# Four small loads on 32 partitions each become two on 64, and SyncE waits for the last eight loads in a no-operation

## The chip, the cores and the metric

The kernel runs on one core of one Trainium2 chip. The metric is the device time of one execution in microseconds (us); lower is better. A profile of one execution gives the span from its first to its last recorded instruction, which is a little shorter than the device time.

## The reference

The kernel computes one decoding step of a layer with two branches. Branch A is attention over a sliding window of the last 4096 cached positions, with 32 query heads on 8 key and value heads of size 128. Branch B is a gated linear unit with 1792 hidden values. A scalar gate mixes the two. Everything is bf16, and there is one token with 512 values.

```python
x = A_x                                              # 1 x 1 x 512
g = sigmoid((x * gate_w).sum(-1))
q = (x @ wq).reshape(1, 1, 32, 128)                  # wq 512 x 4096
k, v = last W = 4096 positions of the caches         # each 8 x 4096 x 128
p = softmax(q . k * 128 ** -0.5)
a = (p . v).reshape(1, 1, 4096) @ wo                 # wo 4096 x 512
h = sigmoid(x @ w_gate) * (x @ w_up)                 # both 512 x 1792
b = h @ w_down                                       # 1792 x 512
out = g * a + (1 - g) * b
```

With one token there is no reuse of weights or caches. All 30.67 MB of weights, keys and values are read once from HBM.

## The kernel before

SyncE issues all the large loads, in the order in which they are used: wq, four loads of keys, w_gate, w_up, four loads of values, two loads of wo, and four pieces of w_down whose sizes fall to the end. The row p of w_up in SBUF holds the four rows 4p to 4p+3 of the matrix. Its main load takes all of each partition but the last three quarters of the fourth row. Those 128 remainders of 1344 values (2688 B) go into a tile of their own, `wx_sb`, of 64 partitions and two halves h, through four small loads.

```python
P = 128; DC = 4; F = 1792; FQ = 448; NP = 64; NJ = 14
WD_SPLIT = (0, 8, 11, 13, 14)
dq = nc.sync
wq_sb = big.tile([P, DC, HQ * DH], BF16, name="wq_sb", tag="big")
dq.dma_start(wq_sb[:], wq_v)

def load_pair(t, cache, a, n0=0, n1=NP):
    dq.dma_start(t[:, n0:n1, :]..., cache[0, 2 * a:2 * a + 2, SBASE:SBASE + W, :]...)

kn = []
for a in range(HP):                                  # 4 loads of keys, 2 MB each
    kn.append(blk.tile([P, NP, P], BF16, name="kn", tag="blk"))
    load_pair(kn[a], A_k_cache, a)
# ... wg_sb
FX = 3 * FQ
LM = DC * F - FX
dq.dma_start(wu_sb[:].rearrange("p c f -> p (c f)")[:, 0:LM],
             B_w_up.rearrange("(p c) f -> p (c f)", c=DC)[:, 0:LM])
wx_sb = const.tile([64, 2, FX], BF16, name="wx_sb")
wx_v = B_w_up.rearrange("(h b j i c) f -> h b i j c f", h=2, b=2, j=4, i=8)[:, :, :, :, DC - 1, F - FX:F]
for h in range(2):
    for b in range(2):
        dq.dma_start(wx_sb[32 * b:32 * b + 32, h, :], wx_v[h, b])

vv = []                                              # 4 loads of values, in the buffers of the keys
for a in range(HP):
    vv.append(blk.tile([P, NP, P], BF16, name="vv", tag="blk"))
    load_pair(vv[a], A_v_cache, a)
# ... wo_sb in two loads
for j0, j1 in zip(WD_SPLIT[:-1], WD_SPLIT[1:]):
    dq.dma_start(wd_sb[:, j0:j1, :], wd_v[:, j0:j1, :])
```

The order of the small rows on the partitions has to agree with the order of the values of x that multiply them. These are picked from x with the same pattern, put on the partitions by two tiny matmuls, and used as stationary operand where the product with w_up comes to the last row:

```python
for h in range(2):
    nc.vector.tensor_copy(xp[:, h, :].rearrange("o (b i j) -> o b i j", b=2, j=4),
                          xr[:, 0, :].rearrange("o (h b j i c) -> o h b i j c", h=2, b=2, j=4, i=8)[:, h, :, :, :, DC - 1])
    nc.tensor.matmul(xx_ps[:, h:h + 1], lhsT=xp[:, h, :], rhs=ident[0:1, 0:1], ...)
# ...
if w == 1 and c == DC - 1 and j >= 1:
    for h in range(2):
        nc.tensor.matmul(g_out, lhsT=xx[:, h:h + 1].to_broadcast([64, 32]),
                         rhs=wx_sb[:, h, (j - 1) * FQ:j * FQ], start=False, stop=(h == 1))
```

After the loads come the scores (DVE transposes the keys, PE multiplies them with the queries), the softmax, the product with the values (`pv_ps`), the product with w_up, and at the end the two output products, which add to one tile `a_ps`: 64 matmuls with wo and 28 with w_down. DVE and ScalarE copy half of `a_ps` each into `res`, and ScalarE issues the output transfer.

Completion of the loads is counted on eight semaphores in turn. A load that takes a semaphore first waits for the load that had it before, eight loads earlier.

Of the kernel before, what the change touches and what calls it, by code (L numbers as in the profile page):

```python
# [17 lines left out]
def kernel(  # L18
# [14 lines left out]
    nc = tc.nc  # L33
# [3 lines left out]
    DC = D // P  # L37
# [5 lines left out]
    W = min(4096, max(256, Sk // 4))  # L43
    KB = W // P
    SBASE = Sk - W
    F = B_w_gate.shape[1]
    NJ = F // P
    N_OUT = A_wo.shape[1]
    NC_O = HQ * DH // P
# [7 lines left out]
    NP = 2 * KB  # L57
# [15 lines left out]
    xr = const.tile([1, 2, D], BF16, name="xr")  # L73
    nc.scalar.dma_start(xr[:, 0, :], A_x[0, :, :])
    nc.scalar.dma_start(xr[:, 1, :], gate_w.rearrange("(o n) -> o n", o=1))

    dq = nc.sync
    wq_sb = big.tile([P, DC, HQ * DH], BF16, name="wq_sb", tag="big")
    wq_v = A_wq.rearrange("(p c) n -> p c n", c=DC)
    dq.dma_start(wq_sb[:], wq_v)  # L80


    def load_pair(t, cache, a, n0=0, n1=NP):
        dq.dma_start(t[:, n0:n1, :].rearrange("p n d -> p (n d)"),  # L84
                     cache[0, 2 * a:2 * a + 2, SBASE:SBASE + W, :]
                     .rearrange("y (x n) d -> x y n d", n=NP)[:, :, n0:n1, :].rearrange("x y n d -> x y (n d)"))

    kn = []
    for a in range(HP):
        kn.append(blk.tile([P, NP, P], BF16, name="kn", tag="blk"))  # L90
        load_pair(kn[a], A_k_cache, a)
# [5 lines left out]
    FX = 3 * FQ  # L97
# [1 line left out]
    dq.dma_start(wu_sb[:].rearrange("p c f -> p (c f)")[:, 0:LM],  # L99
                 B_w_up.rearrange("(p c) f -> p (c f)", c=DC)[:, 0:LM])  # L100
    wx_sb = const.tile([64, 2, FX], BF16, name="wx_sb")
    wx_v = B_w_up.rearrange("(h b j i c) f -> h b i j c f", h=2, b=2, j=4, i=8)[:, :, :, :, DC - 1, F - FX:F]
    for h in range(2):
        for b in range(2):
            dq.dma_start(wx_sb[32 * b:32 * b + 32, h, :], wx_v[h, b])

    vv = []
    for a in range(HP):
        vv.append(blk.tile([P, NP, P], BF16, name="vv", tag="blk"))
        load_pair(vv[a], A_v_cache, a)  # L110

    wo_sb = big.tile([P, NC_O, N_OUT], BF16, name="wo_sb", tag="big")
    wo_v = A_wo.rearrange("(p c) n -> p c n", c=NC_O)
    for c0 in (0, NC_O // 2):
        dq.dma_start(wo_sb[:, c0:c0 + NC_O // 2, :], wo_v[:, c0:c0 + NC_O // 2, :])

    wd_sb = w14.tile([P, NJ, N_OUT], BF16, name="wd_sb", tag="w14")
    wd_v = B_w_down.rearrange("(p j) n -> p j n", j=NJ)
    for j0, j1 in zip(WD_SPLIT[:-1], WD_SPLIT[1:]):
        dq.dma_start(wd_sb[:, j0:j1, :], wd_v[:, j0:j1, :])  # L120


    identf = const.tile([P, P], F32, name="identf")
# [26 lines left out]
    xx_ps = ps_m.tile([64, 2], F32, name="xx_ps", tag="m")  # L150
    xp = const.tile([1, 2, 64], BF16, name="xp")
    for h in range(2):
        nc.vector.tensor_copy(xp[:, h, :].rearrange("o (b i j) -> o b i j", b=2, j=4),
                              xr[:, 0, :].rearrange("o (h b j i c) -> o h b i j c", h=2, b=2, j=4, i=8)[:, h, :, :, :, DC - 1])
        nc.tensor.matmul(xx_ps[:, h:h + 1], lhsT=xp[:, h, :], rhs=ident[0:1, 0:1],
                         start=True, stop=True, skip_group_check=True)
    xT = const.tile([P, DC], BF16, name="xT")
# [216 lines left out]
```

## Time and profile before

| | |
|---|---|
| device time | 80.44 us, median of 3 runs (80.42 to 80.53) |
| span of the profiled execution | 78.7 us, run of 80.39 us |
| granted TensorE clock, mean | 0.973 |
| PE, DVE, ACT busy | 52.5, 38.8, 10.9 us |
| read from HBM | 30.67 MB, 390 GB/s over the span |

The page names PE (TensorE matmul), PEld (its weight load), DVE (VectorE), ACT (ScalarE), POOL (GpSimd), and SPq (SyncE's sequencer, which issues the loads). L105 is line 105 of the kernel, the four small loads. L369 is the end of the program. A DMA's line is named by its destination and source. The page's DMA issues say what each load carries, in the order in which they were costliest:

```profile
## 6 DMA issues: line engine op xcount, KB each, us to landing
kn<-in_A_k_cache_dram SPq DMA_DIRECT2D x4, 2048.0 KB, 27.2
vv<-in_A_v_cache_dram SPq DMA_DIRECT2D x4, 2048.0 KB, 19.1
wq_sb<-in_A_wq_dram SPq DMA_DIRECT2D x1, 4096.0 KB
wo_sb<-in_A_wo_dram SPq DMA_DIRECT2D x2, 2048.0 KB
wg_sb<-in_B_w_gate_dram SPq DMA_DIRECT2D x1, 1792.0 KB
wu_sb<-in_B_w_up_dram SPq DMA_DIRECT2D x1, 1456.0 KB
```

The four small loads have 84.0 KB each. A chip core has 16 DMA engines; a large load is spread over all of them, and the DMA share in the views is the mean busy share of the 16.

### The profile page before, as it was taken

The numbers are of one execution on the slowest core, as the hardware profiler recorded it, in microseconds if no ns is written. First come the engines' busy times: TensorE is split into PE (matmuls) and PEld (weight loads), VectorE is DVE, ScalarE is ACT, GpSimd is POOL, SyncE is SP. The second block draws the span as 40 slices with busy tenths as digits, with TensorE's granted clock in tenths as the row PEclk, the third lists the DMA queues.
The fourth block names the chain that finished last, engine by engine and source line by source line (L and its number), as shares of the span: only waits on it lengthen the run. The fifth ranks groups of instructions, "written<-read, shape, count | busy, mean of one in ns | idle before, by whom it ended". The sixth has DMA issues, their size and how long they took to land.

```text
span 78.7 us, 798 instructions
## 1 busy us (share of the span) xinstructions
PE 52.5 (67%) x314; PEld 23.6 (30%) x314; DVE 38.8 (49%) x52; ACT 10.9 (14%) x20; POOL 3.3 (4%) x10
## 2 busy tenths in 40 slices
PE   0200094999905788898887307999996799567650
PEld 0200041344302333333332202344341345345420
DVE  1600920029869999999986349962000000690020
ACT  2400000247651000000002191000000002000010
POOL 7900000000000000000000000000000000000000
PEclk9999999999999999999999995699999999999997
DMA  7779799999999999999999999999999999999710
GB/s 184 300 316 533 316 483 391 408 425 458 441 408 416 425 474 416 386 437 417 438 410 426 441 416 441 408 433 441 416 433 433 424 425 433 416 391 409 290 42 1
DMA packets 2616, 30.71 MB, mean 390 GB/s; under 512 B 307, under 2 KB 438, under 8 KB 822
## 3 DMA queue, kind: packets, MB, share of 16 engines
q1 hardware_dynamic: 2608, 30.67, 92.9%
q8 instruction: 2, 0.03, 0.2%
q10 hardware_dynamic: 6, 0.00, 0.0%
HBM read 30.67 MB, written 0.00 MB: 390 GB/s over the span
## 4 chain that ended last, share of the span: by engine, by line
DMA 93%; SPq 2%; PE 1%; DVE 1%; issue 0%
DMA wd_sb<-in_B_w_down_dram 36%; DMA kn<-in_A_k_cache_dram 32%; DMA vv<-in_A_v_cache_dram 24%; SPq L84 2%; PE a_ps L290 1%; DVE res L341 1%; SPq L80 0%
## 5 line engine op out<-in xcount | busy, mean ns | idle before, releaser
L299 PE MATMUL pv_ps<-vv,eT 128*32 128x512 bf16 x64 | 15.9, 405 | 4.1 <-DVE eT L271 2.8
L227 PE MATMUL S_ps<-kT,qbig 128*128 128x512 bf16 x64 | 15.2, 378 | 5.0 <-DVE qbig L216 2.8
L188 DVE STREAM_TRANSPOSE kT<-kn 128x2048 f32<-128x2048 f32 x8 | 17.8, 2282 | 0.0
L227 PEld LDWEIGHTS <-qbig 128*128 128x128 bf16 x64 | 6.1, 97 | 14.1 <-issue 4.2
L299 PEld LDWEIGHTS <-eT 128*32 128x32 bf16 x64 | 6.2, 102 | 12.9 <-issue 4.2
L200 PE MATMUL q_ps<-wq_sb,xT 128*128 128x512 bf16 x32 | 8.8, 442 | 1.2 <-DMA wq_sb<-in_A_wq_dram 1.2
L318 DVE TENSOR_TENSOR oT<-o_ps,rb 128x32 bf16<-128x32 f32 x1 | 0.2, 191 | 13.5 <-PE o_ps L316 13.5
L205 DVE STREAM_TRANSPOSE qtT<-q_sb 128x512 f32<-128x512 f32 x4 | 2.7, 700 | 6.9 <-ACT q_sb L202 6.9
L182 PE MATMUL S_ps<-ident,other 2*128 2x512 bf16 x4 | 2.0, 611 | 5.8 <-DVE other L140 5.8
L202 ACT CAST q_sb<-q_ps 128x512 bf16<-128x512 f32 x8 | 4.7, 585 | 7.0 <-PE q_ps L200 7.0
L200 PEld LDWEIGHTS <-xT 128*128 128x128 bf16 x32 | 3.5, 111 | 6.8 <-issue 4.2
L290 PE MATMUL a_ps<-wo_sb,oY 128*1 128x256 bf16 x64 | 3.8, 272 | 1.5 <-DMA wo_sb<-in_A_wo_dram 1.2
L290 PEld LDWEIGHTS <-oY 128*1 128x1 bf16 x64 | 2.7, 83 | 3.1 <-issue 1.4
L271 DVE STREAM_TRANSPOSE eT<-e_sb 128x1024 bf16<-128x1024 bf16 x2 | 2.4, 1224 | 1.9 <-ACT e_sb L269 1.9
L254 ACT ACTIVATE sge<-gu_ps 128x448 f32<-128x448 f32 x1 | 0.5, 543 | 18.9 <-PE gu_ps L243 18.9
L309 ACT COPY pv_sb<-pv_ps 128x512 f32<-128x512 f32 x1 | 0.6, 585 | 17.7 <-PE pv_ps L299 17.7
L341 DVE CAST res<-a_ps 1x256 bf16<-1x256 f32 x1 | 0.4, 412 | 5.2 <-PE a_ps L290 5.2
L281 DVE RECIPROCAL sg<-sge 128x448 f32<-128x448 f32 x1 | 3.0, 2952 | 0.0
L165 DVE TENSOR_TENSOR gpr<-xr 1x512 f32<-1x512 bf16 x1 | 0.7, 679 | 4.6 <-DMA xr<-in_gate_w_dram 4.6
L249 DVE TENSOR_REDUCE pm<-S_ps 128x1 f32<-128x1024 f32 x2 | 2.4, 1208 | 0.9 <-PE S_ps L227 0.9
L290 PE MATMUL a_ps<-wd_sb,hT 128*1 128x256 bf16 x28 | 2.1, 271 | 0.8 <-DMA wd_sb<-in_B_w_down_dram 0.8
L148 PE MATMUL xt_ps<-ident,xr 1*128 1x1 bf16 x4 | 0.3, 165 | 3.5 <-POOL ident L126 3.5
(62 smaller groups left out, 31.0 us busy)
## 6 DMA issues: line engine op xcount, KB each, us to landing
kn<-in_A_k_cache_dram SPq DMA_DIRECT2D x4, 2048.0 KB, 27.2
vv<-in_A_v_cache_dram SPq DMA_DIRECT2D x4, 2048.0 KB, 19.1
wq_sb<-in_A_wq_dram SPq DMA_DIRECT2D x1, 4096.0 KB
wo_sb<-in_A_wo_dram SPq DMA_DIRECT2D x2, 2048.0 KB
wg_sb<-in_B_w_gate_dram SPq DMA_DIRECT2D x1, 1792.0 KB
wu_sb<-in_B_w_up_dram SPq DMA_DIRECT2D x1, 1456.0 KB
wd_sb<-in_B_w_down_dram SPq DMA_DIRECT2D x1, 1024.0 KB
wd_sb<-in_B_w_down_dram SPq DMA_DIRECT2D x1, 384.0 KB
```

The lines of the kernel that those rows point to most:

```text
L84: dq.dma_start(t[:, n0:n1, :].rearrange("p n d -> p (n d)"), cache[0, 2 * a:2 * a + 2, SBASE:SBASE + W, :] .rearrange("y (x n) d -> x y n ...
L182: nc.tensor.matmul(S_ps[u // 2][:, u % 2, :], lhsT=other[:].rearrange("p o y u -> p (o y u)"), rhs=ident[0:2, 0:2].rearrange("p (o y) -> p ...
L188: nc.vector.transpose(t[:].bitcast(F32), kn[a][:, v * KB:(v + 1) * KB, :] .rearrange("p n d -> p (n d)").bitcast(F32))
L200: nc.tensor.matmul(q_ps[:], lhsT=xT[:, c:c + 1].to_broadcast([P, P]), rhs=wq_sb[:, c, ks], start=(c == 0), stop=(c == DC - 1))
L202: nc.scalar.copy(q_sb[:, ks], q_ps[:])
L205: nc.vector.transpose(qtT[:].bitcast(F32)[:, kq], q_sb[:].bitcast(F32)[:, kq])
L227: nc.tensor.matmul(S_ps[v][:, hb, :], lhsT=q_st[:, a, dhi, :, t], rhs=k_v[:, hb * 16:(hb + 1) * 16, dhi, :, t], start=False, stop=(a == HP ...
L249: nc.vector.tensor_reduce(pm2[:, v:v + 1], S_ps[v][:].rearrange("p a b -> p (a b)"), axis=AX.X, op=ALU.max)
L271: nc.vector.transpose(eT[:, :, v * KB:(v + 1) * KB, :].rearrange("p a n r -> p n a r"), e_sb[:, v, :].rearrange("p (n a r) -> p n a r", a= ...
L281: nc.vector.reciprocal(sg[:], sge[:])
L290: nc.tensor.matmul(a_ps[32 * i:32 * i + 1, i, 0:HN], lhsT=lhsT, rhs=rhs[:, i * HN:(i + 1) * HN], start=start, stop=stop)
L299: nc.tensor.matmul(pv_ps[32 * a:32 * a + 32, :, :], lhsT=eT[:, a, 4 * m:4 * m + 4, :].rearrange("p n r -> p (n r)"), rhs=vv[a][:, 4 * m:4 ...
```

## The change

The four small loads of 32 partitions become two of 64, one for each half h. The eight values of i remain the slowest dimension of the source, so that the rows stay on eight DMA engines, now with eight rows for each engine and load. The order of the values of x follows. The second part collects the load instructions in a list and puts a no-operation into SyncE's stream, after the last issue, that depends on the last eight of them (two of vv, two of wo, four of w_down); the closing waits of the program then need not name these loads again. The purpose is fewer loads and fewer waits at the end. What is computed stays the same.

```diff
+    loads = []
...
     def load_pair(t, cache, a, n0=0, n1=NP):
-        dq.dma_start(t[:, n0:n1, :].rearrange("p n d -> p (n d)"),
...
+        loads.append(dq.dma_start(t[:, n0:n1, :].rearrange("p n d -> p (n d)"),
...
     wx_sb = const.tile([64, 2, FX], BF16, name="wx_sb")
-    wx_v = B_w_up.rearrange("(h b j i c) f -> h b i j c f", h=2, b=2, j=4, i=8)[:, :, :, :, DC - 1, F - FX:F]
+    wx_v = B_w_up.rearrange("(h j i c) f -> h i j c f", h=2, j=8, i=8)[:, :, :, DC - 1, F - FX:F]
     for h in range(2):
-        for b in range(2):
-            dq.dma_start(wx_sb[32 * b:32 * b + 32, h, :], wx_v[h, b])
+        dq.dma_start(wx_sb[:, h, :], wx_v[h])
...
-        dq.dma_start(wd_sb[:, j0:j1, :], wd_v[:, j0:j1, :])
+        loads.append(dq.dma_start(wd_sb[:, j0:j1, :], wd_v[:, j0:j1, :]))
+
+
+    seen = dq.nop()
+    for load in loads[-8:]:
+        tc.add_manual_dep(seen.ins, load.ins.name,
+                          mybir.DependencyInfo(mybir.DependencyClass.Sync, mybir.DependencyReason.DATA), reason="loads ended")
...
     for h in range(2):
-        nc.vector.tensor_copy(xp[:, h, :].rearrange("o (b i j) -> o b i j", b=2, j=4),
-                              xr[:, 0, :].rearrange("o (h b j i c) -> o h b i j c", h=2, b=2, j=4, i=8)[:, h, :, :, :, DC - 1])
+        nc.vector.tensor_copy(xp[:, h, :].rearrange("o (i j) -> o i j", i=8),
+                              xr[:, 0, :].rearrange("o (h j i c) -> o h i j c", h=2, j=8, i=8)[:, h, :, :, DC - 1])
```

More of the change, by code (lines that the diff above doesn't have):

```diff
@@ L83, in load_pair @@
     def load_pair(t, cache, a, n0=0, n1=NP):
-        dq.dma_start(t[:, n0:n1, :].rearrange("p n d -> p (n d)"),
-                     cache[0, 2 * a:2 * a + 2, SBASE:SBASE + W, :]
-                     .rearrange("y (x n) d -> x y n d", n=NP)[:, :, n0:n1, :].rearrange("x y n d -> x y (n d)"))
+        loads.append(dq.dma_start(t[:, n0:n1, :].rearrange("p n d -> p (n d)"),
+                                  cache[0, 2 * a:2 * a + 2, SBASE:SBASE + W, :]
+                                  .rearrange("y (x n) d -> x y n d", n=NP)[:, :, n0:n1, :].rearrange("x y n d -> x y (n d)")))
     kn = []
@@ L114 @@
     for c0 in (0, NC_O // 2):
-        dq.dma_start(wo_sb[:, c0:c0 + NC_O // 2, :], wo_v[:, c0:c0 + NC_O // 2, :])
+        loads.append(dq.dma_start(wo_sb[:, c0:c0 + NC_O // 2, :], wo_v[:, c0:c0 + NC_O // 2, :]))
     wd_sb = w14.tile([P, NJ, N_OUT], BF16, name="wd_sb", tag="w14")
```

## The prediction

> **What bounds the kernel now.** I read the shares of the chain that ended last, then the DMA lines, then that chain in order of time, and last the same span in half-microsecond windows. From the page, the shares by engine and by line, and the DMA totals:
>
> ```profile
> DMA packets 2616, 30.71 MB, mean 390 GB/s; under 512 B 307, under 2 KB 438, under 8 KB 822
> q1 hardware_dynamic: 2608, 30.67, 92.9%
> DMA 93%; SPq 2%; PE 1%; DVE 1%; issue 0%
> DMA wd_sb<-in_B_w_down_dram 36%; DMA kn<-in_A_k_cache_dram 32%; DMA vv<-in_A_v_cache_dram 24%; SPq L84 2%; PE a_ps L290 1%; DVE res L341 1%; SPq L80 0%
> ```
>
> 93% of the chain is transfer, nearly all on the queue of SyncE; PE is busy 67% of the span and DVE 49%, neither is the limit. The end of the chain in order of time (start, length, what):
>
> ```profile
> 46.84 28.67 DMA wd_sb<-in_B_w_down_dram
> 75.51 0.04 issue
> 75.55 0.66 PE a_ps L290 x6
> 76.20 0.40 DVE res L341
> ```
>
> The last piece of w_down lands at 75.51 us of a span of 78.7 us. Six matmuls, the copy of the result and the output transfer follow, 3.2 us that this change does not touch. So the time moves with the landing of the last load and with little else. The windows (length, busy PE, PEld, DVE, ACT, POOL, PE clock, DMA share, GB/s) show how the stream runs in its middle and how it ends:
>
> ```profile
> 56.00:58.00 2.00, 1.96 (x10) 0.69 (x8) 0.00 (x0) 0.00 (x0) 0.00 (x0) 1.00 1.00 426
> 72.50:73.00 0.50, 0.50 (x14) 0.41 (x10) 0.00 (x0) 0.00 (x0) 0.00 (x0) 1.00 1.07 428
> 73.50:74.00 0.50, 0.10 (x2) 0.09 (x3) 0.00 (x0) 0.00 (x0) 0.00 (x0) 1.00 0.77 295
> 74.00:74.50 0.50, 0.50 (x12) 0.40 (x10) 0.00 (x0) 0.00 (x0) 0.00 (x0) 1.00 0.64 242
> 74.50:75.00 0.50, 0.50 (x13) 0.31 (x10) 0.00 (x0) 0.00 (x0) 0.00 (x0) 1.00 0.63 229
> 75.00:75.50 0.50, 0.36 (x6) 0.15 (x3) 0.00 (x0) 0.00 (x0) 0.00 (x0) 1.00 0.24 82
> ```
>
> The DMA engines are full (share 1.00, 426 GB/s, that is 26.6 GB/s for each of 16) until about 73.2 us, and then only some of them work for two more microseconds. Which ones? The 307 packets under 512 B are completion marks: 17 loads from SyncE on 16 engines give 272, the four small loads of w_up on 8 engines give 32, the three transfers on the other queue give 3, together 307. On 16 engines the small loads would have given 64, together 339. So wx_sb moves on 8 engines alone: 128 rows of 2688 B are 344 KB, 43 KB for each of the eight, 43 KB / 26.6 GB/s = 1.6 us of work that the other eight do not have. The engines with the small rows are those that end last, at 75.2 to 75.5 us; the packet records of the trace put six of the others at 73.7 to 74.0. The remaining two end with the late ones: two packets of instructions of 16 KB (q8 on the page) hold up one engine each. **Anything that lengthens the small rows therefore lengthens the kernel almost one for one; shortening them helps only until those two engines are left.**
>
> The waits of SyncE's own queue, at the end of the program and at the v loads (total, times, longest), and its issues (start, time):
>
> ```profile
> SPq L369 <- DMA wd_sb<-in_B_w_down_dram: 23.3, 3, 21.8
> SPq L84 <- DMA kn<-in_A_k_cache_dram: 8.4, 2, 4.2
> SPq L369 <- DMA out_dram<-res: 1.1, 1, 1.1
> SPq L369 <- DVE res L341: 1.1, 1, 1.1
> ```
>
> ```profile
> 12.95 10.46 SPq L105 DMA_DIRECT2D wx_sb<-in_B_w_up_dram  x4
> 27.70 14.67 SPq L84 DMA_DIRECT2D vv<-in_A_v_cache_dram  x4
> ```
>
> SyncE is through with its last issue at 51.7 us and has nothing to do but wait. At the end it is held by the w_down pieces, then by DVE's copy, then by the output, in that order.
>
> [...]
>
> **The change part by part.** *Rows and engines.* The bytes are the same, 344 KB on 8 engines, 16 rows each. Before, load b of half h puts rows 4i to 4i+3 of a block of 32 partitions on engine i[...]. After, 64 partitions are cut in 8 for the 8 values of i. [...] I take it that engine i gets partitions 8i to 8i+7. [...] No run here shows this split of 64; it is my inference.
>
> *Its cost.* A 2688 B row takes 0.103 to 0.107 us in the packet records, so 16 rows take 1.67 us. [...] They are not in step: the eight engines reach the small rows between 39.59 and 39.94 us, neighbours in time some 0.1 us apart. In a set of four rows (0.42 us alone) the one that is ahead by d has d to itself and shares the rest, so a set takes 0.84 - d. With d = 0.05 to 0.15 four sets cost 4 x (0.27 to 0.37) = 1.1 to 1.5 us. About 1.3 us[...].
>
> *Two loads fewer.* Each of the eight engines writes two marks less: the packet records show about 0.01 us each, so -0.02 us. SyncE saves two issues of 0.7 us (10.46 us for four include the waits between), not on the path. The slots of eight semaphores shift by two: the first v load waited for the third k load until 27.6 us, now for the first one and for DVE's second transposition, which ends about 26.8; so it is issued about 0.9 us earlier. The later v loads also wait for DVE or an earlier k load. All this is hidden: vv lands 19 us after its issue because some 14 us of queue are ahead of it (its landing at 46.8 less 5 us for its own 128 KB per engine).
>
> *The no-operation.* Its eight waits come after the last issue, on SyncE alone, and are over with the last w_down piece at 75.5. Until 76.6 DVE's copy holds SyncE anyway, and until about 77.6 the output. Before, the same waits stood in the closing block, also ahead of those two. One wait instruction and a branch of perhaps 0.1 us (my guess) then have 1.1 us to hide in: 0.
>
> *Sum.* 80.44 - 0.02 + 0 + (0, or about 1.3) = 80.4 or 81.7.
>
> **The rivals.** *No sharing, nothing moves:* 80.4. For it: all rows still go to the same 8 engines with the same bytes, and the diff intends own partitions. [...] *Sharing in step:* 82.0 to 82.1, 2% slower; against it the 0.1 us offsets. *The closing waits come out:* if SyncE's last waits cost time after the output, taking six of the eight away would give some tenths, 80.1; but the waits view shows the output as the last to release it. *The earlier v loads fill gaps:* only if the stream starved, and from 38 to 72 us the share stays at 0.93 or more: 0 to -0.1. PE taking over as the bound: it would need to lose its slack before w_down; it follows the v loads, and these shift by no more than w_down does.
>
> **Range and chances.** [...] Between 80.4 and 81.7 I put 81.2 us; 80.2 to 82.1 should hold it 8 times in 10. Slower by over 2% (above 82.05) needs sharing in step: 0.13. Faster by over 2% (below 78.8) has no source, since two engines end at 75.4 without the small rows: 0.02. Within 2%: 0.85.
>
> **What would show it.** 2600 packets with 291 under 512 B confirm eight engines and two loads. Sharing shows in the window 39.5 to 43.5 us: DMA bytes fall well under 426 GB/s, the first v load's landing goes from 46.8 to about 48, and the last w_down landing to about 76.8 with a longer stretch at half share ahead of it. Without sharing the last landing stays at 75.5 and the half-share stretch at 2 us. If the stretch from the last landing to the end differs from 3.2 us, I was wrong on the no-operation. If the landing moves earlier than 75.2, I was wrong on what ends last.

## The result, and the profile after

| | before | after |
|---|---|---|
| device time, median | 80.51 us (80.42 to 81.83, 6 runs) | 81.46 us (81.25 to 81.87, 6 runs) |
| span of the profiled execution | 78.7 us | 79.6 us |
| first load (wq) landed | 12.95 us | 13.21 us |
| last piece of w_down landed | 75.51 us | 76.38 us |
| from there to the end of the span | 3.2 us | 3.2 us |

The ratio of after to before is 1.0125, with an interval of 1.0098 to 1.0152. Some executions of most of these kernels take 1.5 to 2.2% longer than the others of the same kernel (81.83 us here, of the kernel before); medians and ranges have them in, ratios do not. The change costs 1.0 us of device time, and what was meant to save loads and waits saves nothing. The DMA totals and the shares of the chain that ended last, from the page of the changed kernel:

```profile
DMA packets 2600, 30.71 MB, mean 386 GB/s; under 512 B 291, under 2 KB 422, under 8 KB 806
...
DMA 77%; PE 13%; DVE 6%; ACT 1%; issue 0%
DMA wd_sb<-in_B_w_down_dram 36%; DMA vv<-in_A_v_cache_dram 25%; DMA wq_sb<-in_A_wq_dram 16%; PE q_ps L206 12%; DVE kT L194 3%; DVE qbig L222 2%; DVE qtT L211 1%; PE a_ps L296 1%; ACT q_sb L208 1%; DVE res L347 1%
```

There are 16 packets less, all of them completion marks: two loads fewer on eight engines each. The bytes are the same. The chain now passes through PE and DVE for 19%, where before it was 93% transfer. That is no new bound. It is another route back through the same early stretch, as the chain in order of time shows (start, length, what):

```profile
25.49 2.32 DVE kT L194
...
27.83 19.87 DMA vv<-in_A_v_cache_dram
...
47.72 28.66 DMA wd_sb<-in_B_w_down_dram
76.38 0.04 issue
76.43 0.64 PE a_ps L296 x6
77.07 0.40 DVE res L347
```

The first v load is now released by DVE's transposition of the keys (L194) instead of by the landing of a k load, and so the walk back goes through DVE and PE. The load itself still waits in a full queue for most of its 19.87 us. From the v landing on, both chains are alike: 28.66 us here and 28.67 us before to the last landing, then the same tail. So the loss is already there at 47.70 us, where before the landing was at 46.84. The windows of the changed kernel over the small rows and over the end (length, busy PE, PEld, DVE, ACT, POOL, PE clock, DMA share, GB/s):

```profile
39.50:41.50 2.00, 1.71 (x9) 0.70 (x8) 2.00 (x2) 0.00 (x0) 0.00 (x0) 1.00 1.06 348
41.50:43.50 2.00, 2.00 (x23) 0.78 (x21) 1.11 (x2) 0.00 (x0) 0.00 (x0) 1.00 1.04 360
...
75.50:76.00 0.50, 0.50 (x12) 0.31 (x9) 0.00 (x0) 0.00 (x0) 0.00 (x0) 1.00 0.51 180
```

And the same four microseconds of the kernel before:

```profile
39.50:41.50 2.00, 1.71 (x9) 0.68 (x7) 1.60 (x2) 0.00 (x0) 0.00 (x0) 1.00 1.06 425
41.50:43.50 2.00, 1.32 (x19) 0.33 (x16) 1.38 (x2) 0.54 (x1) 0.00 (x0) 1.00 1.02 434
```

The DMA share is over 1.00 in all four lines: on average no engine is idle, before or after. Yet the changed kernel moves 348 and 360 GB/s where before it was 425 and 434. Engines that are busy and move less are being held in their packets, whose times follow below. The loss is (77 + 74) GB/s x 2 us = 302 KB, which at the stream's 426 GB/s is 0.7 us. Outside this stretch the streams run alike: in the packet records of the trace the changed kernel is 28 KB behind the kernel before at 39.4 us, 331 KB at 43.5 us and 339 KB at 60 us. At the end, half of the engines are still busy at 75.5 to 76.0 us (share 0.51), when the kernel before is through.

In the packet records, the small rows of 2688 B take 107 ns each before, and 134 ns on average after; along one engine they swing between 107 and about 200 ns. The first 16 KB packets of v that follow take up to 948 ns, against 614 ns undisturbed. These records are what the experiments below are read by, together with the windows. They do not name the engine, but one small row follows another closely (in both kernels the next starts, in the median, 3 ns ahead of the recorded end of the one before), and so an engine can mostly be followed.

### The profile page after: what moved, and what is told of

It is laid out like the page before. It is cut to its first block, busy times and chain, and to the rows that moved or that the text cites. A ratio compares the mean times of both kernels' runs of the same rounds, so it can differ in the third digit from the quotient of the medians.

```text
span 79.6 us, 798 instructions
## 1 busy us (share of the span) xinstructions
PE 55.7 (70%) x314; PEld 25.0 (31%) x314; DVE 38.9 (49%) x52; ACT 10.9 (14%) x20; POOL 3.3 (4%) x10
## 4 chain that ended last, share of the span: by engine, by line
DMA 77%; PE 13%; DVE 6%; ACT 1%; issue 0%
DMA wd_sb<-in_B_w_down_dram 36%; DMA vv<-in_A_v_cache_dram 25%; DMA wq_sb<-in_A_wq_dram 16%; PE q_ps L206 12%; DVE kT L194 3%; DVE qbig L222 2%; DVE qtT L211 1%; PE a_ps L296 1%; ACT q_sb L208 1%; DVE res L347 1%
## 5 line engine op out<-in xcount | busy, mean ns | idle before, releaser
L233 PE MATMUL S_ps<-kT,qbig 128*128 128x512 bf16 x64 | 16.3, 404 | 3.9 <-DVE qbig L222 2.8
L194 DVE STREAM_TRANSPOSE kT<-kn 128x2048 f32<-128x2048 f32 x8 | 17.8, 2279 | 0.0
L206 PE MATMUL q_ps<-wq_sb,xT 128*128 128x512 bf16 x32 | 9.5, 469 | 1.3 <-DMA wq_sb<-in_A_wq_dram 1.3
L296 PE MATMUL a_ps<-wo_sb,oY 128*1 128x256 bf16 x64 | 5.3, 346 | 0.3 <-DVE oY L330 0.3
L296 PEld LDWEIGHTS <-oY 128*1 128x1 bf16 x64 | 3.6, 104 | 2.6 <-DVE oY L330 1.1
L188 PEld LDWEIGHTS <-other 2*128 2x128 bf16 x4 | 0.6, 157 | 6.2 <-DVE other L146 5.9
```

The source lines that it names most:

```text
L188: nc.tensor.matmul(S_ps[u // 2][:, u % 2, :], lhsT=other[:].rearrange("p o y u -> p (o y u)"), rhs=ident[0:2, 0:2].rearrange("p (o y) -> p ...
L194: nc.vector.transpose(t[:].bitcast(F32), kn[a][:, v * KB:(v + 1) * KB, :] .rearrange("p n d -> p (n d)").bitcast(F32))
L206: nc.tensor.matmul(q_ps[:], lhsT=xT[:, c:c + 1].to_broadcast([P, P]), rhs=wq_sb[:, c, ks], start=(c == 0), stop=(c == DC - 1))
L233: nc.tensor.matmul(S_ps[v][:, hb, :], lhsT=q_st[:, a, dhi, :, t], rhs=k_v[:, hb * 16:(hb + 1) * 16, dhi, :, t], start=False, stop=(a == HP ...
L296: nc.tensor.matmul(a_ps[32 * i:32 * i + 1, i, 0:HN], lhsT=lhsT, rhs=rhs[:, i * HN:(i + 1) * HN], start=start, stop=stop)
```

## The experiments

Theory: the partitions that the small rows go to make the difference. 64 partitions cut in eight put engine i, as I take it, on partitions 8i to 8i+7, and engines then hold each other up. Both are my estimate, which no trace of before shows. The rivals: the no-operation costs the time; fewer, larger loads on shared semaphores cost it; or the new order of the source rows in HBM costs it. Two forms of the theory are told apart further on: the rows are slow only while engines hold each other up (A1), or every row is slow whose engine writes, as I take it, other partitions than in the kernel before (A2). All ratios are to the kernel before, run on the same chip in the same set, with 95% intervals.

### The no-operation alone

The kernel before, its four small loads kept, plus:

```diff
+    seen = dq.nop()
+    for load in loads[-8:]:
+        tc.add_manual_dep(seen.ins, load.ins.name, ...)
```

> The kernel before with the no-operation alone; the four small loads as they were. Theory A (the small rows' partitions make the difference): ratio to the kernel before 1.000, within 0.002; last landing and the 3.2 us after it as before. Rival B (the no-operation and its waits cost the time): ratio about 1.012, with a longer stretch between the last landing and the end.

Measured: 80.57 us, ratio 0.9998 (0.9966 to 1.0030). The waits of SyncE's queue in this kernel (total us, times, longest), L124 being the no-operation and L376 the end of the program:

```profile
SPq L124 <- DMA wd_sb<-in_B_w_down_dram: 23.7, 2, 23.5
...
SPq L376 <- DMA out_dram<-res: 1.1, 1, 1.1
...
SPq L376 <- DVE res L348: 0.5, 1, 0.5
```

The waits for w_down have moved from the closing block to the no-operation. The output is still awaited for 1.1 us after everything else, as before. The wait for DVE's copy is 0.5 us where it was 1.1: SyncE gets there later, and still too early. The no-operation neither costs nor saves.

### Two loads of 64, without the no-operation

> The two loads of 64 partitions alone, without the no-operation. Theory A: ratio 1.010 to 1.015, as the whole change; the two windows 39.5 to 43.5 us move about 350 GB/s instead of 430. Rival B: ratio 1.000.

Measured: ratio 1.0127 (1.0102 to 1.0152), the same as the whole change; it rests on two executions, of 81.49 and 81.54 us. For the windows, one more execution was profiled:

> The two loads of 64 partitions alone once more, for a profile beside the others. Theory A: the two windows 39.5 to 43.5 us move 340 to 370 GB/s, last landing 76.2 to 76.5.

It took 81.36 us; the windows of 39.5 to 43.5 us moved 322 and 366 GB/s (the first less than the 340 that I had expected), and the last load landed at 76.37 us, with rows at 149 ns on average. The loads alone carry the whole effect.

### Two loads, each on a block of 32 partitions

The same number of loads, the same bytes, the same source rows in the same order on the same engines; only the destination differs, 32 partitions with two pieces each.

```diff
-    wx_v = B_w_up.rearrange("(h j i c) f -> h i j c f", h=2, j=8, i=8)[:, :, :, DC - 1, F - FX:F]
-    for h in range(2):
-        dq.dma_start(wx_sb[:, h, :], wx_v[h])
+    wx_v = B_w_up.rearrange("(b m i c) f -> b i m c f", b=2, m=8, i=8)[:, :, :, DC - 1, F - FX:F]
+    for b in range(2):
+        dq.dma_start(wx_sb[32 * b:32 * b + 32, :, :], wx_v[b])
```

(The no-operation is left out too; the order of x follows.)

> Two loads of eight rows for each engine, from the same source rows in the same order as the whole change has them, but written to 32 partitions each (4i to 4i+3 of a block for engine i, two halves side by side). Only the destination partitions differ from the two loads of 64. Theory A: ratio 0.998 to 1.001, small rows at 107 ns a packet-row as before, no dip below 420 GB/s. Rival C (two larger loads instead of four, or the earlier turn of the semaphores, cost the time): ratio about 1.012. Rival D (reading the rows from HBM in this order is slow): about 1.012.

Measured: 80.62 us, ratio 1.0009 (0.9976 to 1.0043), rows at 107 ns, last landing 75.45 us, with the same 2600 packets as after. The windows of this kernel:

```profile
39.50:41.50 2.00, 1.71 (x8) 0.68 (x7) 1.53 (x2) 0.00 (x0) 0.00 (x0) 1.00 1.06 433
41.50:43.50 2.00, 1.27 (x19) 0.38 (x18) 1.38 (x2) 0.54 (x1) 0.00 (x0) 1.00 1.02 434
```

The dip is gone. Between this kernel and the two loads of 64, only the destination partitions differ, and they make 1.2% (1.0009 against 1.0127). That rules out the number and size of the loads, the semaphores they take, and the order of the rows in HBM.

### Half the dose

Half h = 0 in one load of 64 partitions, h = 1 in the two old loads of 32.

```diff
+    dq.dma_start(wx_sb[:, 0, :], wx_w[0])            # wx_w: the pattern of after
+    for b in range(2):
+        dq.dma_start(wx_sb[32 * b:32 * b + 32, 1, :], wx_v[1, b])
```

> Half the dose: the small rows of the half h=0 in one load of 64 partitions, those of h=1 in two of 32 as before. Theory A: half of the effect, ratio 1.005 to 1.007. If the placing of one load is enough to set the whole cost, 1.012.

Measured: 81.05 us, ratio 1.0078 (1.0053 to 1.0104). The first window falls to 307 GB/s, the second is back at 449, and the last load lands at 76.00 us. The loss follows the dose: half of the rows bring some 0.6 of it, a little more than I had expected, and the 1.012 of the other case lies outside the interval.

### On partitions 64 to 127

Four loads of 32 partitions as before, but on partitions 64 to 127, while the other eight engines have their stream of v.

```diff
-            dq.dma_start(wx_sb[32 * b:32 * b + 32, h, :], wx_v[h, b])
+            dq.dma_start(wx_sb[64 + 32 * b:64 + 32 * b + 32, h, :], wx_v[h, b])
```

> The kernel before with its four small loads on partitions 64 to 127 instead of 0 to 63. [...] the eight engines need 3.3 us for the small rows instead of 1.67 us, their end moves by 1.6 us, ratio 1.020; the other eight lose as much in the same stretch. If which partitions an engine writes has no effect: 1.000.

Measured: 81.99 us, ratio 1.0180 (1.0152 to 1.0207), last landing 77.49 us in a profiled execution of 82.37. The windows:

```profile
39.50:41.50 2.00, 1.71 (x9) 0.68 (x8) 1.97 (x2) 0.00 (x0) 0.00 (x0) 1.00 1.10 264
41.50:43.50 2.00, 2.00 (x22) 0.72 (x20) 1.26 (x2) 0.00 (x0) 0.00 (x0) 1.00 1.08 289
```

This is the clearest case. From 40.1 us on the rows take 209 ns on average, twice 107; those that start in the first 0.4 us, up to 39.95 us, still take 107. The 16 KB packets of the other eight engines take about 1219 ns at the same time, twice 611. Each side runs at half its speed here, and the load that was moved is not the only one to pay.

### Moved by 16 partitions

The four loads on partitions 16 to 79 (16 to 47, then 48 to 79), the other rows of a 96-partition tile zeroed.

> The kernel before with its four small loads moved by 16 partitions (16 to 79; the other rows of a tile of 96 are set to zero and multiply zeros). [...] Theory A1 [...]: the first block costs nothing, of the second block half the engines are slowed, one set of four rows for each half: at most 2 x 0.42 us for those four engines, ratio 1.000 to 1.010, and in the trace rows at 107 ns and a part at about 210. Theory A2 [...]: all rows slow, ratio 1.012 or more.

Measured: 81.67 us, ratio 1.0151 (1.0121 to 1.0181), windows of 314 and 336 GB/s, last landing 76.50 us. More than expected; by its ratio alone this run speaks for theory A2. Its packet records speak against all rows being slow: the rows take 140 to 221 ns from 40.0 to 41.0 us, most of them 107 to 135 ns from 41.1 to 41.4 us, and the last ones 158 to 218 ns again. So the rows are slow in two stretches and not throughout. I had counted on the second, for half of the engines; the first I had left out. It follows the change-over from the main w_up load, which the engines do not reach at once (in the kernel before the eight start their rows within 0.35 us); that engines are in each other's way there is my reading. The next pair shows a slow stretch at this place alone.

### On one block of 32 partitions

Twins with four loads on one block of 32 partitions and four pieces per partition, at partitions 0 to 31, or 16 to 47. Both need four small matmuls per column block in place of two; both also write the reciprocal of the gate in place.

```diff
+    BASE = 16                                        # 0 in the twin
...
-            dq.dma_start(wx_sb[32 * b:32 * b + 32, h, :], wx_v[h, b])
+            dq.dma_start(wx_sb[BASE:BASE + 32, 2 * h + b, :], wx_v[h, b])
```

> The four small loads of the kernel before, all to partitions 16 to 47 (four places side by side, the other rows zero, 12 small matmuls for the last row instead of 6). [...] Compared with its twin on partitions 0 to 31. A1 [...]: within 0.3 us of the twin, rows at 107 ns but for the first and last 0.4 us. A2 [...]: rows at 140 ns and more, 0.8 us or more over the twin.

> The twin of the run above: the same program with all four small loads on partitions 0 to 31[...]. A1 and A2 both: rows at 107 ns, ratio to the kernel before 0.998 to 1.004 (the six more matmuls of about 0.35 us lie ahead of the wait for the last loads).

Measured: 81.64 us, ratio 1.0115 (1.0086 to 1.0144) on partitions 16 to 47, and 81.53 us, 1.0119 (1.0079 to 1.0159) on 0 to 31. The twin on 0 to 31 should have been within 0.4% of before, and wasn't. The windows, first of the kernel on 16 to 47:

```profile
39.00:40.50 1.50, 1.21 (x7) 0.49 (x5) 1.50 (x2) 0.00 (x0) 0.00 (x0) 1.00 0.94 324
40.50:42.00 1.50, 1.50 (x8) 0.48 (x5) 0.72 (x1) 0.00 (x0) 0.00 (x0) 1.00 1.14 431
```

then of the twin on 0 to 31:

```profile
39.00:40.50 1.50, 1.21 (x7) 0.48 (x5) 1.50 (x2) 0.00 (x0) 0.00 (x0) 1.00 1.04 420
40.50:42.00 1.50, 1.50 (x15) 0.53 (x16) 0.62 (x2) 0.00 (x0) 0.00 (x0) 1.00 1.02 421
```

The twin on 0 to 31 has no dip, and rows at 107 ns throughout. Its time is lost elsewhere: the page of either twin has a DMA queue that the kernel before has not.

```profile
q8 instruction: 2, 0.03, 0.2%
q14 instruction: 1, 0.01, 0.0%
```

One more packet of instructions, 8 KB, is fetched at 57.7 us, in the midst of the stream, where the kernel before fetches none; I take it that the longer program needs it. In both twins one engine then ends last, alone: the share is 0.06, one of 16, for the last half microsecond up to a landing at 76.14 us on 0 to 31, and for the last 0.9 us up to 76.78 on 16 to 47. So the times of this pair say little of the partitions, because a late engine hides what the others lost. The packet records show which engine it is. In the twin on 0 to 31 the additional packet takes 0.33 us and the 16 KB packet behind it 1.27 us instead of 0.61, so that its engine, one of the nine that are late already, falls back by 1.0 us. Its next completion mark comes 0.57 us after the last of the others (61.71 and 61.14 us), and at the end one engine is 0.57 us behind the rest (76.00 and 75.43 us by the marks). On 16 to 47 the two distances are 0.93 us. The twin's profiled execution took 81.03 us, the fastest of four; the others, of 81.37 to 81.80 us, have no profile. The windows say more: on 16 to 47 the rate is down to 324 GB/s in the change-over alone, where rows that start between 39.9 and 40.3 us take up to 231 ns, and then it is 431 GB/s with rows at 107. These partitions are not slow in themselves, against A2: rows to the same 32 partitions are slow for a time and then not. That two engines are in each other's way in the change-over is the reading that fits, not one that a record shows.

### No small rows at all

w_up in one load of 1792 KB on 16 engines; the small tile and its matmuls are left out, and the last row is multiplied like the others. The same work is done.

```diff
-    FX = 3 * FQ
+    FX = 0
```

> The kernel before without small loads: w_up in one load of 1792 KB on 16 engines, and the last row multiplied like the others. It tests the step on what ends last. If the two engines with an instruction packet are what is left: they end about 76.0 us (0.8 us later than with the rows moved off them), ratio 1.005 to 1.010; the others end at 74.6. If the eight engines with small rows alone set the end: landing 74.6, ratio 0.990.

Measured: 81.30 us, ratio 1.0101 (1.0070 to 1.0132), last landing 76.15 us. The end of the stream:

```profile
74.50:75.00 0.50, 0.42 (x8) 0.35 (x9) 0.00 (x0) 0.00 (x0) 0.00 (x0) 1.00 0.13 49
75.00:75.50 0.50, 0.50 (x12) 0.35 (x7) 0.00 (x0) 0.00 (x0) 0.00 (x0) 1.00 0.13 47
```

A share of 0.13 is 2 of 16 engines, as many as there are instruction packets of 16 KB (1.06 and 1.10 us each); they end 1.2 and 1.6 us after the other fourteen. In the packet records these two can be followed: with the packet behind it, which is slower too (1.11 us instead of 0.61 behind the first one of the kernel before), each instruction packet puts its engine back by 1.5 us. With the small rows on eight other engines, they end at about 75.4; with 344 KB spread over all 16, each gets 21.5 KB more, 0.8 us at 26.6 GB/s, and 75.4 + 0.8 = 76.2 is where the kernel ends.

### Plain order of rows, 16 engines on 64 partitions

Two loads of 64 partitions with the rows in their natural order, so that 16 engines take part (2616 packets, as counted ahead), and the no-operation left out.

```diff
+    wx_v = B_w_up.rearrange("(h r c) f -> h r c f", h=2, r=64)[:, :, DC - 1, F - FX:F]
```

> Two loads of 64 partitions with the rows in plain order, so that the slowest source dimension is 64 and all 16 engines share the small rows; 339 less 32 or 307 packets under 512 B (two loads of 16 marks). The bytes per engine are those of one load of w_up for all[...]. A1: rows at about 210 ns throughout, 8 rows for each engine in 1.7 us instead of 0.84; the engines with an instruction packet end at 76.8, ratio 1.016 to 1.02. [...] like one load of w_up, ratio 1.010.

Measured: 82.57 us, ratio 1.0245 (1.0212 to 1.0279), windows of 267 and 289 GB/s, rows at 195 ns on average, last landing 77.49 us. With all 16 engines writing to these 64 partitions, the rows take nearly twice their 107 ns. The loss is larger than I had expected. The rows themselves lose 8 x (195 - 107) ns = 0.70 us on each engine; what I had not counted is the first 16 KB packet behind them, which on 14 of the 16 engines takes 1140 to 1320 ns, against 614.

### The dose over the runs

The bytes missing in 39.5 to 43.5 us against the kernel before, (425 + 434 - the two rates) x 2 us, beside the ratio:

| small rows | missing KB | ratio |
|---|---|---|
| two loads, on blocks of 32 | about 0 | 1.0009 |
| half in 64, half in 32 | 206 | 1.0078 |
| the change | 302 | 1.0125 |
| two loads of 64 alone | 342 | 1.0127 |
| four loads, moved by 16 | 418 | 1.0151 |
| four loads on 64 to 127 | 612 | 1.0180 |
| 16 engines on 64 partitions | 606 | 1.0245 |

With one inversion, at the two largest, the order of the ratios is that of the bytes missing. The last row has a second cost in it: with the rows on all 16 engines it is the two engines with instruction packets that end last, which alone makes 1.0101 in the kernel without small rows, so that some 1.4 of its 2.45% are left for the slower rows. The table leaves out the no-operation alone (about 0 missing, 0.9998), the twins, which the additional packet makes late (164 KB missing on 16 to 47, none on 0 to 31), and the kernel without small rows.

## Why the prediction was right, and where a size was off

The prediction was 81.2 us with a range of 80.2 to 82.1, and "within 2%" as the likely class. The result, 81.46 us, lies in the range and the class.

- **Bound.** Right. The last w_down landing moved by 0.87 us, the device time by 1.0 us, and the tail stayed at 3.2 us.
- **Eight engines carry the small rows and end last.** Right: 2600 packets, 291 under 512 B, as said. In the packet records of the changed kernel six engines finish the first v load at 45.19 to 45.64 us and the eight with the small rows at 46.84 to 47.22, counted from the start of the span.
- **Two further engines end at 75.4 for their instruction packets, so shortening the rows gains little.** Right; the kernel without small rows ends at these two, at 76.15 us. In that kernel each of the two packets of q8, of 16 KB, puts its engine back by 1.5 us. In a stream as full as this one (DMA share 1.00 and 426 GB/s at 56 to 58 us in the kernel before) that delay is still there at the end: the two engines trail by 1.2 and 1.6 us.
- **The cut of 64 partitions in eight, and engines that hold each other up.** This was my inference, and no trace of before showed it. The measurements agree with it: rows of 209 ns on partitions 64 to 127 and of 195 ns with 16 engines on 64 partitions, 107 ns in two loads on blocks of 32, and a loss that only the destination partitions switch on (1.0127 against 1.0009). No record names the partitions of one packet, so that engine i has exactly 8i to 8i+7 is the reading that fits, not one seen directly; nor is it shown which engines hold each other up, and by what.
- **Cost of the sharing: four sets x (0.42 - d), 1.1 to 1.5 us.** The estimate takes it that two engines run at half speed while both are at their rows, which the trace of before does not show; the 0.42 us of four rows and the offsets d are from that trace. The step was off in size. The small rows lost 16 x (134 - 107) ns = 0.43 us on each engine, and the first v packets behind them another 0.3 to 0.4 us, which I had not counted: together 0.7 to 0.8 us. In the formula that is d = 0.23 us, and not the 0.05 to 0.15 that I took from the offsets of the engines' starts. I had also read the offsets too evenly: the eight engines start their rows at 39.46 to 39.80 us from the start of the span (the prediction has them 0.13 us later), and of the seven gaps four are 0.07 to 0.10 us and three under 0.01. Nor does the delay run set by set. The rows that start in the first 0.5 us, up to 40.0 us, still take 107 to 112 ns on all eight engines, though the estimate has them slowed as soon as a second engine joins; then rows take up to 212 ns, and the delay goes on into the v packets. Why it sets in late is not settled. The last landing came 0.87 us later; of this, 0.07 us was there ahead of the small rows (28 KB less moved by 39.4 us), so that the packets account for the profiled pair to within 0.1 us. The profiled execution of the changed kernel is the fastest of its six, 81.25 us; by the medians of six runs the cost is 1.0 us, a little under the low end of the term.
- **Weighing 0 against 1.3 us.** The prediction put 81.2 between the two cases; given sharing, its sum was 81.7, and the result is 81.46. That 81.2 came so close is in part luck: it was a mean of two cases, and the one that happened came out smaller than its sum.
- **v loads issued 0.9 us earlier.** Wrong in this profile: the first went out at 27.83 us, where before it was 27.70. DVE's second transposition, which I had put at an end of 26.8 us, ended at 27.81, behind queries that PE finished later. With the two loads on blocks of 32 it did go out at 26.80. Neither shows in the time: v landed at 46.78 us there, and at 46.84 before.
- **No-operation 0, two loads fewer 0.** Right: ratio 0.9998 for the first alone, and 1.0009 for two loads on blocks of 32.

The window of 39.5 to 43.5 us, the landing of v "to about 48" (47.70) and the last landing "about 76.8" (76.38) came as the signs for sharing said, the last one smaller.

## What to carry to other kernels

When a load is spread over only some of the DMA engines, look at its destination, and try another; here that choice alone was worth 1.2% (1.0009 on blocks of 32 partitions, 1.0127 on 64), with the same bytes, number of engines and number of loads. With the stream full, fewer loads (1.0009) and fewer waits on the issuing engine (0.9998) were worth nothing here: ask which engine's last packet lands last, and what it carries that the others don't. A dip of GB/s at a DMA share of 1.00 says that packets take longer; here it was 348 GB/s at a share of 1.06, with rows of 134 ns instead of 107. It was found by windows, not by totals.

## What the runs showed that I had not expected

- Packets of instructions take part in the race of the DMA engines: in the kernel without small rows, two engines trail by 1.2 and 1.6 us and alone make it 1% slower than the kernel before, which had put its small rows on other engines. A third packet, of 8 KB, put an engine that was late already back by 1.0 us, and this engine set the end in the twin on partitions 0 to 31, whose windows show no loss of rate. That is shown for its profiled execution; the whole +1.2% of its four runs is not accounted for.
- In the changed kernel, the eight engines that carry no small rows also lost about 0.7 us in the same stretch: their 16 KB packets took 670 to 890 ns, against 614. The estimate had only the eight with small rows hold each other up. The kernel moved by 16 partitions shows the like: the eight rows that start between 40.7 and 40.9 us all take 182 to 221 ns, though I had expected at most four of the eight engines to be slowed. Whether the delay comes from something that all engines have in common was not tried and stays open.
- Rows on partitions 16 to 47 ran at 107 ns and 431 GB/s once the change-over was past: writing these partitions does not cost by itself.
